# Order of the output stage, the spread of softmax reciprocals and twenty small memsets in a fused attention and GEGLU kernel

## Chip, cores and metric

The kernel runs on one core of a Trainium2 chip. The metric is the device time in microseconds, the median of several runs.

## What is computed

A sequence of 2048 rows of 512 (bf16) is normalised. One branch is attention with 32 heads of 16, in which each position looks at 8 keys, two positions apart, behind it. The other is a gated MLP of width 1792. Their product is added to the input.

```
xn = layernorm(x)
q, k, v = split(xn @ wqkv)                    # 32 heads of 16
idx = pos - 2 * arange(8);  mask = idx >= 0
attn = softmax(where(mask, q . k[idx] / 4, -1e9))
s = (attn . v[idx]) @ wo
y = (gelu(xn @ w_gate) * (xn @ w_up)) @ w_down
out = x + s * silu(y)
```

## The kernel before

The rows are handled in four chunks j of 512 columns (four tiles of 128 rows each). The order of the work is written out by hand: every engine runs its own instructions in the order in which the program emits them. The main loops (L531 to L541) go through, for each chunk, 14 slices of the gated MLP (`glu`, L394), then the 12 projections of the next chunk (`qkv`, L257: four q, four k, four v), then the four output tiles of this chunk (`down`, L407). The pieces of the attention are hung between these with `at(key, fn, ...)`, and `run` emits them ahead of the slice, projection or tile of that key. So `at(("qkv", 1, 10), av_sums, 0)` puts the sums of chunk 0 ahead of projection 10 of chunk 1.

The attention of a chunk goes through these steps:

- `qk_product` (L290): VectorE multiplies q by k shifted by 2w, for each of the 8 taps w, into a buffer `pk`. `pk` and `pv` share eight buffers.
- `logits` (L298): TensorE sums the products over the 16 positions of a head with the constant matrix `dsum` (32 columns wide, four of them side by side on the array) into `L_ps`; ScalarE takes the exponential into `E`. For chunk 0 GpSimd zeroes what lies before the first row.
- `denominators` (L318): TensorE sums `E` over the taps with the constant `hsum`, also 32 columns wide, into `den_ps`; VectorE takes the reciprocal into `rs`, a 128x128 tile.
- `av_product` (L358): VectorE multiplies `E` by the shifted v (`v_arr`, read back from the DRAM tensor `vT` by `load_v`), eight times, into `pv`.
- `av_sums` (L369): TensorE sums these over the taps with `hsum` into `o_ps`, 32 matmuls of 32 columns. The matmuls read the eight products one after the other. `o_ps` and `L_ps` share one PSUM buffer of four banks.
- The reciprocals must be spread from a tile of 128x128 to one of 128x512, `rb`. `spread_by_dma` (L347) does it for chunks 0 to 2: a store of `rs` to the DRAM tile `rs_d`, then four loads. `spread_reciprocals` (L336) does it for chunk 3 with four matmuls by a constant `spread` into `sp_ps` and a copy by ScalarE.
- `divide` (L384): VectorE multiplies `o_ps` by `rb`, in two halves, into `oT`.

`down` computes for a tile of rows y (14 matmuls by w_down) and, directly behind it, s (4 matmuls of `oT` by wo); ScalarE takes silu of y into `sl`; VectorE makes m = s * sl and o_t = m + x; a DMA stores it. The very last tile is done in two halves of 256 columns.

The PSUM pool `mm` has four buffers, which g, u, y, s, the projections, `den_ps` and `sp_ps` take in turn. All DMAs are issued by SyncE (SP), one after the other; an issue that waits holds back those behind it. The constants `dsum`, `hsum` and `spread` are made by GpSimd in `sum_constants` (L145), which is emitted ahead of the second half of the first projections. Before it on GpSimd stand the `pow` of the norms of tiles 4 to 7, behind it those of tiles 8 to 15.

Of the kernel before, what the change touches and what calls it, by code (L numbers as in the profile page):

```python
# [8 lines left out]
ALU = mybir.AluOpType  # L9
AF = mybir.ActivationFunctionType  # L10
BF16 = mybir.dt.bfloat16
F32 = mybir.dt.float32

P = 128
H = 32
# [6 lines left out]
TQ = 512  # L22
# [6 lines left out]
def kernel(  # L29
# [13 lines left out]
    nc = tc.nc  # L43
    B, S, D = A_x.shape
    DF = B_w_gate.shape[1]
    NT, NC, NF, NJ = S // P, D // P, DF // P, S // TQ
    TPQ = TQ // P
    SV = PAD + S
    x2d, out2d = A_x[0], out[0]
# [3 lines left out]
    def pool(name, bufs, **kw):  # L53
        return ctx.enter_context(tc.tile_pool(name=name, bufs=bufs, **kw))

    const = pool("const", 1)
# [8 lines left out]
    op = pool("op", 1)  # L65
    sm = pool("sm", 3)
    sm2 = pool("sm2", 2)
    sm4 = pool("sm4", 4)
    xnp = pool("xnp", 6)
    dram = pool("dram", 1, space=bass.MemoryType.DRAM)  # L70
    mm = pool("mm", 4, space=bass.MemoryType.PSUM)
# [3 lines left out]
    x_sb = big.tile([P, NT, D], BF16, name="x_sb")  # L75
# [3 lines left out]
    wd_sb = wts.tile([P, NF, D], BF16, name="wd_sb")  # L79
    wo_sb = wts.tile([P, NC, D], BF16, name="wo_sb")  # L80
    vT = dram.tile([D, SV], BF16, name="vT")
    rs_d = [dram.tile([P, P], BF16, name=f"rs_d{j}") for j in range(NJ - 1)]

    def load_x(t, n=1):
        nc.sync.dma_start(
# [21 lines left out]
    def load_late_weights():  # L107
# [13 lines left out]
    ident = const.tile([P, P], BF16, name="ident")  # L121
    make_identity(nc, ident[:])
    nc.sync.dma_start(
        out=vT.rearrange("(k p) n -> p k n", p=P)[:, :, 0:PAD],
        in_=zpad[:],
    )

    def band(dst, lo_base, hi_base, step, mult, n):

        nc.gpsimd.affine_select(  # L130
            out=dst, in_=dst, pattern=[[-step, n]], compare_op=ALU.is_ge, fill=0.0,
            base=lo_base, channel_multiplier=mult,
        )
        nc.gpsimd.affine_select(
            out=dst, in_=dst, pattern=[[step, n]], compare_op=ALU.is_gt, fill=0.0,
            base=hi_base, channel_multiplier=-mult,
        )


    hsum = const.tile([P, H], BF16, name="hsum")  # L140
    spread = const.tile([P, 4, P], BF16, name="spread")

    dsum = const.tile([P, NC, H], BF16, name="dsum")

    def sum_constants():  # L145

        nc.gpsimd.memset(dsum[:], 0.0)
        for c in range(NC):
            nc.gpsimd.memset(dsum[:, c, 8 * c : 8 * c + 8], 1.0)
            band(dsum[:, c, 8 * c : 8 * c + 8], 0, 16, 16, 1, 8)  # L150
        for j in range(WL):
            nc.gpsimd.tensor_copy(
                out=hsum[H * j : H * (j + 1), :],
                in_=ident[H * j : H * (j + 1), H * j : H * (j + 1)],
            )
        nc.gpsimd.memset(spread[:], 0.0)
        for q in range(4):
            for j in range(4):
                nc.gpsimd.tensor_copy(
                    out=spread[H * q : H * (q + 1), q, H * j : H * (j + 1)],  # L160
                    in_=ident[H * q : H * (q + 1), H * q : H * (q + 1)],
                )

    xnT = {}
    k_sb = big.tile([P, NC, PAD + S], BF16, name="k_sb")
# [89 lines left out]
    st = [dict(pk={}, pv={}) for _ in range(NJ)]  # L255

    def qkv(j, fo, i0=0, n=TQ, ps=None):  # L257
        which, c = divmod(fo, NC)
        if fo == 0 and i0 == 0:
            st[j]["q"] = qp.tile([P, NC, TQ], BF16, name="q_sb")  # L260
        if ps is None:
            ps = mm.tile([P, n], F32, name="qkv_ps", tag="mm")[:]
            project(ps, wqkv_sb, fo * P, j, i0, n)
        if which == 0:
            nc.scalar.activation(out=st[j]["q"][:, c, i0 : i0 + n], in_=ps, func=AF.Copy)  # L265
        elif which == 1:
            lo = PAD + j * TQ + i0
            nc.scalar.activation(out=k_sb[:, c, lo : lo + n], in_=ps, func=AF.Copy)  # L268
        else:
            vst = sm4.tile([P, TQ], BF16, name="vst")  # L270
            nc.scalar.activation(out=vst[:], in_=ps, func=AF.Copy)  # L271
            lo = PAD + j * TQ
            nc.sync.dma_start(out=vT[c * P : (c + 1) * P, lo : lo + TQ], in_=vst[:])
# [44 lines left out]
    def denominators(j):  # L318
# [14 lines left out]
            nc.vector.reciprocal(out=rs[:], in_=den[:])  # L333
        st[j]["rs"] = rs

    def spread_reciprocals(j):  # L336
        sp = mm.tile([P, TQ], F32, name="sp_ps", tag="mm")
        for q in range(4):
            nc.tensor.matmul(
                sp[:, q * P : (q + 1) * P], lhsT=spread[:, q, :], rhs=st[j]["rs"][:],  # L340
                start=True, stop=True,
            )
        rb = op.tile([P, TQ], F32, name="rb")
        nc.scalar.activation(out=rb[:], in_=sp[:], func=AF.Copy)
        st[j]["rb"] = rb

    def spread_by_dma(j):  # L347

        nc.sync.dma_start(out=rs_d[j][:, :], in_=st[j]["rs"][:])
        rb = op.tile([P, TQ], BF16, name="rbd")  # L350
        for i in range(WL):
            nc.sync.dma_start(
                out=rb[H * i : H * (i + 1), :].rearrange("h (q i) -> h q i", q=4),
                in_=rs_d[j].rearrange("(q h) i -> h q i", h=H),
            )
        st[j]["rb"] = rb
# [47 lines left out]
        nc.vector.tensor_tensor(out=h[:], in0=ge[:], in1=u[:], op=ALU.mult)  # L404
        st[j][fc] = h

    def down(j, tt):  # L407
        t = j * TPQ + tt
        halves = [slice(0, D // 2), slice(D // 2, D)] if t == NT - 1 else [slice(0, D)]
        n = D // len(halves)  # L410
        sl = sm2.tile([P, D], BF16, name="sl")
        o_t = sm4.tile([P, D], BF16, name="o_t")
        for i, cols in enumerate(halves):
            y = mm.tile([P, n], F32, name="y_ps", tag="mm")
            for fc in range(NF):
                nc.tensor.matmul(  # L416
                    y[:],
                    lhsT=st[j][fc][:, tt * P : (tt + 1) * P],
                    rhs=wd_sb[:, fc, cols],
                    start=(fc == 0),  # L420
                    stop=(fc == NF - 1),
                )
            nc.scalar.activation(out=sl[:, cols], in_=y[:], func=AF.Silu)  # L423
            s = mm.tile([P, n], F32, name="s_ps", tag="mm")
            for g in range(NC):
                nc.tensor.matmul(  # L426
                    s[:],
                    lhsT=st[j]["oT"][:, g, tt * P : (tt + 1) * P],
                    rhs=wo_sb[:, g, cols],
                    start=(g == 0),  # L430
                    stop=(g == NC - 1),
                )
            m = sm2.tile([P, n], BF16, name="m")
            nc.vector.tensor_tensor(out=m[:], in0=s[:], in1=sl[:, cols], op=ALU.mult)  # L434
            nc.vector.tensor_tensor(out=o_t[:, cols], in0=m[:], in1=x_sb[:, t, cols], op=ALU.add)
            nc.sync.dma_start(out=out2d[t * P : (t + 1) * P, cols], in_=o_t[:, cols])


    side = {}
# [1 line left out]
    def at(key, fn, *args):  # L441
        side.setdefault(key, []).append((fn, args))

    def run(stage, j, i):
        for fn, args in side.get((stage, j, i), ()):
            fn(*args)
# [13 lines left out]
        at(("glu", 0, w), qk_product, 0, w)  # L460
    at(("glu", 0, 9), logits, 0)
    for i in range(8):
        at(("glu", 0, 12 + i) if i < 2 else ("qkv", 1, (0, 1, 3, 4, 5, 6)[i - 2]),
           av_product, 0, i // 2, i % 2)
    at(("qkv", 1, 3), denominators, 0)
    at(("qkv", 1, 3), spread_by_dma, 0)
    at(("qkv", 1, 10), av_sums, 0)
    at(("qkv", 1, 10), divide, 0)

    for j in range(1, NJ):  # L470
        for w in range(W):
            early = j > 1 and w < 3
            at(("qkv", j, 9 + w) if early else ("down", j - 1, w // 3), qk_product, j, w)
        for i in range(TPQ):
            at(("down", j - 1, i), load_v, j, [i])
        at(("glu", j, 0), logits, j)
        for i in range(8):
            at(("glu", j, 2 + i), av_product, j, i // 2, i % 2)
        at(("glu", j, 11), denominators, j)
        at(("glu", j, 11), av_sums, j)  # L480
        if j + 1 < NJ:
            at(("glu", j, 11), spread_by_dma, j)
            at(("qkv", j + 1, 6), divide, j)
        else:
            at(("glu", j, 12), spread_reciprocals, j)
            at(("glu", j, 13), divide, j)


    HT = TPQ // 2
# [41 lines left out]
    for j in range(NJ):  # L531
        for fc in range(NF):
            run("glu", j, fc)
            glu(j, fc)
        if j + 1 < NJ:
            for i in range(12):
                run("qkv", j + 1, i)
                qkv(j + 1, i)
        for tt in range(TPQ):
            run("down", j, tt)  # L540
            down(j, tt)  # L541
# [1 line left out]
_INS = ['A_x', 'A_wqkv', 'A_wo', 'B_x', 'B_w_gate', 'B_w_up', 'B_w_down']  # L543
_OUTS = [((1, 2048, 512), 'bfloat16')]
# [25 lines left out]
```

The softmax here doesn't subtract the row's maximum and nothing guards it: scores larger than these inputs give would overflow.

## Time and profile before

| | |
|---|---|
| median of 5 runs | 230.37 us (229.94 to 230.49) |
| profiled execution | 230.1 us |
| its span in the profile | 228.4 us |
| mean granted TensorE clock | 0.998 |
| DMA moved | 24.46 MB |

The profile shows one execution. Times in it are microseconds from the start of the span. PE is TensorE's matmul, PEld its weight load, DVE VectorE, ACT ScalarE, POOL GpSimd, SP SyncE; SPq is SP's DMA queue. A row of a timeline has the start, the time covered, the engine, the line of the program, the operation, the tile written and the tiles read, and, in brackets, how long the engine had been idle and what ended that. The chain of waits follows the work that ended last back to the start. The last matmul group of the timeline, an s of 256 columns, starts at 224.25, and the last o_t on VectorE at 225.42. The stores of the reciprocals have 32 KB each and landed in a median of 1.5 us, the twelve loads of rbd in 1.6 to 2.1 us, the stores of vT (128 KB each) in 1.7 to 8.3, the loads of v_arr (520 KB each) in 4.8 to 12.2 with a median of 5.1.

### The profile page before, as it was taken

To read this page: it belongs to the slowest core of one execution; us is meant where nothing else is said; L and a number is where in the kernel's file an instruction comes from. 1 tells how busy PE (TensorE), PEld (TensorE's weight loads), DVE (VectorE), ACT (ScalarE), POOL (GpSimd) and SP (SyncE) were. 2 spreads that over 40 slices of the span, in tenths; PEclk is the share of its full clock that TensorE was granted. 3 is DMA by queue.
4 is the path that set the end of the run, shared out by engine and by line. 5 is a ranking of instruction groups with operands and counts; after the bars stand their busy time and mean duration, and the time that the engine had idled before them with its cause. 6 is when DMAs were issued, how large, how long until landed. Compare 5 with 4: busy or idle time off the path is not lost.

```text
span 228.4 us, 3538 instructions
## 1 busy us (share of the span) xinstructions
PE 223.7 (98%) x1324; PEld 106.6 (47%) x1324; DVE 147.7 (65%) x234; ACT 130.1 (57%) x214; POOL 22.0 (10%) x61
## 2 busy tenths in 40 slices
PE   8999999999999999999999999999999999999993
PEld 6864444444444444444444444444444444444453
DVE  4693996896994298864687179635549429945232
ACT  3779769764413876467621786747632396748211
POOL 1058943000000000110000000000000000000000
PEclk9999999999999999999999999999999999999999
DMA  5999589982468111110287511110147800000001
GB/s 171 357 372 373 135 170 197 234 219 72 120 159 207 45 25 28 26 29 0 92 185 158 138 25 29 26 35 0 46 128 160 202 27 0 0 0 4 23 23 46
DMA packets 30545, 24.46 MB, mean 107 GB/s; under 512 B 10176, under 2 KB 30528, under 8 KB 30528
## 3 DMA queue, kind: packets, MB, share of 16 engines
q1 hardware_dynamic: 30528, 24.24, 41.7%
q8 instruction: 10, 0.16, 0.3%
q14 instruction: 7, 0.06, 0.1%
HBM read 18.61 MB, written 4.31 MB: 100 GB/s over the span
## 4 chain that ended last, share of the span: by engine, by line
PE 96%; ACT 2%; DVE 0%; issue 0%; DVEq 0%
PE y_ps L416 21%; PE u_ps L247 21%; PE g_ps L247 21%; PE qkv_ps L247 18%; PE s_ps L426 6%; PE L_ps L304 3%; PE o_ps L375 3%; PE warm_ps L229 2%; PE q_ps L247 1%; ACT xnT L221 1%; ACT L400 1%; PE tr L212 0%; PE den_ps L324 0%; ACT ge L400 0%; ACT vst L271 0%; DVE m L434 0%
## 5 line engine op out<-in xcount | busy, mean ns | idle before, releaser
L247 PE MATMUL g_ps<-xnT,wg_sb 128*128 128x512 bf16 x224 | 57.6, 379 | 0.0
L247 PE MATMUL u_ps<-xnT,wu_sb 128*128 128x512 bf16 x224 | 57.5, 379 | 0.0
L416 PE MATMUL y_ps<-wd_sb,h 128*128 128x512 bf16 (+1 forms) x238 | 51.2, 366 | 0.0
L404 DVE TENSOR_TENSOR h<-ge,u 128x512 bf16<-128x512 bf16 x56 | 23.8, 425 | 37.2 <-ACT u L402 36.6
L293 DVE TENSOR_TENSOR pk<-q_sb,k_sb 128x2048 bf16<-128x2048 bf16 x32 | 37.8, 1220 | 7.0 <-ACT k_sb L268 7.0
L402 ACT ACTIVATE u<-u_ps 128x512 bf16<-128x512 f32 x56 | 33.5, 599 | 14.7 <-PE u_ps L247 14.7
L400 ACT ACTIVATE ge<-g_ps 128x512 bf16<-128x512 f32 x56 | 33.5, 598 | 14.7 <-PE g_ps L247 14.4
L247 PE MATMUL qkv_ps<-xnT,wqkv_sb 128*128 128x512 bf16 (+1 forms) x208 | 40.9, 355 | 0.0
L361 DVE TENSOR_TENSOR pv<-E,v_arr 128x2048 bf16<-128x2048 bf16 x32 | 38.6, 1217 | 0.0
L416 PEld LDWEIGHTS <-h 128*128 128x128 bf16 x238 | 23.3, 98 | 25.3
L423 ACT ACTIVATE sl<-y_ps 128x512 bf16<-128x512 f32 (+1 forms) x17 | 9.7, 572 | 44.0 <-PE y_ps L416 44.0
L247 PEld LDWEIGHTS <-wu_sb 128*128 128x128 bf16 x224 | 21.9, 98 | 26.7 <-issue 0.3
L247 PEld LDWEIGHTS <-wg_sb 128*128 128x128 bf16 x224 | 21.2, 98 | 27.1 <-issue 3.0
L247 PEld LDWEIGHTS <-wqkv_sb 128*128 128x128 bf16 x224 | 21.7, 98 | 19.7 <-issue 0.7
L434 DVE TENSOR_TENSOR m<-s_ps,sl 128x512 bf16<-128x512 f32 (+1 forms) x17 | 11.2, 658 | 24.2 <-PE s_ps L426 24.1
L426 PE MATMUL s_ps<-wo_sb,oT 128*128 128x512 bf16 (+1 forms) x68 | 16.6, 366 | 0.0
L197 POOL TENSOR_TENSOR rstd<-rstd,mhalf 128x1 f32<-128x1 f32 x12 | 7.6, 636 | 78.0 <-DVE rstd L194 75.8
L271 ACT ACTIVATE vst<-qkv_ps 128x512 bf16<-128x512 f32 x16 | 9.6, 597 | 6.4 <-PE qkv_ps L247 6.4
L268 ACT ACTIVATE k_sb<-qkv_ps 128x512 bf16<-128x512 f32 (+1 forms) x20 | 10.1, 516 | 3.5 <-PE qkv_ps L247 3.2
L265 ACT ACTIVATE q_sb<-qkv_ps 128x512 bf16<-128x512 f32 (+1 forms) x16 | 8.7, 544 | 3.6 <-PE qkv_ps L247 3.3
L426 PEld LDWEIGHTS <-oT 128*128 128x128 bf16 x68 | 6.6, 98 | 7.2
L192 DVE BATCH_NORM_STATS2 stats<-x_sb 128x6 f32<-128x512 bf16 x12 | 8.2, 686 | 1.3 <-DMA x_sb<-in_A_x_dram 1.3
(52 smaller groups left out, 116.8 us busy)
## 6 DMA issues: line engine op xcount, KB each, us to landing
v_arr<-vT SPq DMA_DIRECT2D x16, 520.0 KB, 5.1
vT<-vst SPq DMA_DIRECT2D x16, 128.0 KB, 2.5
out_dram<-o_t SPq DMA_DIRECT2D x15, 128.0 KB, 1.9
wg_sb<-in_B_w_gate_dram SPq DMA_DIRECT2D x2, 896.0 KB, 10.8
wu_sb<-in_B_w_up_dram SPq DMA_DIRECT2D x2, 896.0 KB, 12.9
wd_sb<-in_B_w_down_dram SPq DMA_DIRECT2D x1, 1792.0 KB, 14.0
wqkv_sb<-in_A_wqkv_dram SPq DMA_DIRECT2D x3, 512.0 KB, 4.9
x_sb<-in_A_x_dram SPq DMA_DIRECT2D x3, 512.0 KB, 12.0
```

The costliest lines, as they stand in the source:

```text
L247: nc.tensor.matmul(ps, lhsT=w[:, dk, lo : lo + P], rhs=xnT[j][:, dk, i0 : i0 + n], start=(dk == 0), stop=(dk == NC - 1),)
L268: nc.scalar.activation(out=k_sb[:, c, lo : lo + n], in_=ps, func=AF.Copy)
L271: nc.scalar.activation(out=vst[:], in_=ps, func=AF.Copy)
L293: nc.vector.tensor_tensor(out=pk[:], in0=st[j]["q"][:], in1=k_sb[:, :, off : off + TQ], op=ALU.mult)
L361: nc.vector.tensor_tensor(out=pv[:], in0=st[j]["E"][:, wh, :].unsqueeze(1).to_broadcast([P, 4, TQ]), in1=st[j]["va"][:, 4 * g : 4 * g + 4, ...
L400: nc.scalar.activation(out=ge[:], in_=g_ps[:], func=AF.Gelu_apprx_tanh)
L402: nc.scalar.activation(out=u[:], in_=u_ps[:], func=AF.Copy)
L404: nc.vector.tensor_tensor(out=h[:], in0=ge[:], in1=u[:], op=ALU.mult)
L416: nc.tensor.matmul(y[:], lhsT=st[j][fc][:, tt * P : (tt + 1) * P], rhs=wd_sb[:, fc, cols], start=(fc == 0), stop=(fc == NF - 1),)
L423: nc.scalar.activation(out=sl[:, cols], in_=y[:], func=AF.Silu)
L426: nc.tensor.matmul(s[:], lhsT=st[j]["oT"][:, g, tt * P : (tt + 1) * P], rhs=wo_sb[:, g, cols], start=(g == 0), stop=(g == NC - 1),)
L434: nc.vector.tensor_tensor(out=m[:], in0=s[:], in1=sl[:, cols], op=ALU.mult)
```

## The change

- y and s are split into `down` and `finish`. y of a tile is followed by s of the tile before it; s of a chunk's last tile follows its y. In the last tile of all, y of the first half is followed by s of tile 14 and then by its own s.
- The reciprocals of all four chunks go by DRAM. The function with the matmuls is gone, with the constant `spread`. The store and the four loads are now two functions. In chunk 0 the store is emitted ahead of projection 8 and the loads ahead of projection 10, so that the vT stores of projections 8 and 9 stand between them on SP.
- In chunk 0 `denominators` moves from projection 3 to 8 and `av_sums` from 10 to 8, directly behind it. The products of chunk 0 begin a slice earlier, ahead of glu 11, and end ahead of projection 5 instead of 6.
- The divide of chunk 0 moves from projection 10 to the first output tile, that of chunk 3 from glu 13 to the first output tile. Those of chunks 1 and 2 stay.
- The first three pk products of chunk 1 move from the first output tile to projections 9 to 11, as chunks 2 and 3 have them.
- `sl` now has three buffers of its own (two before), and `o_t` is made for the columns it needs.
- GpSimd gets twenty memsets of one element per partition, all into one tile `filler`, ahead of `dsum`. In the compiled program the first waits for nothing, and each of the other nineteen waits for GpSimd's own previous instruction.

```diff
-    rs_d = [dram.tile([P, P], BF16, name=f"rs_d{j}") for j in range(NJ - 1)]
+    rs_d = [dram.tile([P, P], BF16, name=f"rs_d{j}") for j in range(NJ)]
...
-    spread = const.tile([P, 4, P], BF16, name="spread")
-
     dsum = const.tile([P, NC, H], BF16, name="dsum")
 
+    filler = const.tile([P, 1], F32, name="filler")
+
     def sum_constants():
+
+        for _ in range(20):
+            nc.gpsimd.memset(filler[:], 0.0)
 
         nc.gpsimd.memset(dsum[:], 0.0)
...
-        nc.gpsimd.memset(spread[:], 0.0)
-        for q in range(4):
-            for j in range(4):
-                nc.gpsimd.tensor_copy(
-                    out=spread[H * q : H * (q + 1), q, H * j : H * (j + 1)],
-                    in_=ident[H * q : H * (q + 1), H * q : H * (q + 1)],
-                )
...
+    def store_reciprocals(j):
+        nc.sync.dma_start(out=rs_d[j][:, :], in_=st[j]["rs"][:])
+
     def spread_reciprocals(j):
-        sp = mm.tile([P, TQ], F32, name="sp_ps", tag="mm")
-        for q in range(4):
-            nc.tensor.matmul(
-                sp[:, q * P : (q + 1) * P], lhsT=spread[:, q, :], rhs=st[j]["rs"][:],
-                start=True, stop=True,
-            )
-        rb = op.tile([P, TQ], F32, name="rb")
-        nc.scalar.activation(out=rb[:], in_=sp[:], func=AF.Copy)
-        st[j]["rb"] = rb
-
-    def spread_by_dma(j):
-
-        nc.sync.dma_start(out=rs_d[j][:, :], in_=st[j]["rs"][:])
-        rb = op.tile([P, TQ], BF16, name="rbd")
+
+        rb = op.tile([P, TQ], BF16, name="rb")
         for i in range(WL):
             nc.sync.dma_start(
...
+    def down(j, tt, cols):
+
+        n = cols.stop - cols.start
+        y = mm.tile([P, n], F32, name="y_ps", tag="mm")
...
+        sl = sm.tile([P, n], BF16, name="sl")
+        nc.scalar.activation(out=sl[:], in_=y[:], func=AF.Silu)
+        return sl
+
+    def finish(j, tt, cols, sl):
+
+        t, n = j * TPQ + tt, cols.stop - cols.start
+        s = mm.tile([P, n], F32, name="s_ps", tag="mm")
...
+        m = sm2.tile([P, n], BF16, name="m")
+        nc.vector.tensor_tensor(out=m[:], in0=s[:], in1=sl[:], op=ALU.mult)
+        o_t = sm4.tile([P, n], BF16, name="o_t")
+        nc.vector.tensor_tensor(out=o_t[:], in0=m[:], in1=x_sb[:, t, cols], op=ALU.add)
+        nc.sync.dma_start(out=out2d[t * P : (t + 1) * P, cols], in_=o_t[:])
...
-        at(("glu", 0, 12 + i) if i < 2 else ("qkv", 1, (0, 1, 3, 4, 5, 6)[i - 2]),
+        at(("glu", 0, 11 + i) if i < 3 else ("qkv", 1, (0, 1, 2, 4, 5)[i - 3]),
            av_product, 0, i // 2, i % 2)
-    at(("qkv", 1, 3), denominators, 0)
-    at(("qkv", 1, 3), spread_by_dma, 0)
-    at(("qkv", 1, 10), av_sums, 0)
-    at(("qkv", 1, 10), divide, 0)
+    at(("qkv", 1, 8), denominators, 0)
+    at(("qkv", 1, 8), av_sums, 0)
+    at(("qkv", 1, 8), store_reciprocals, 0)
+    at(("qkv", 1, 10), spread_reciprocals, 0)
+    at(("down", 0, 0), divide, 0)
 
     for j in range(1, NJ):
         for w in range(W):
-            early = j > 1 and w < 3
-            at(("qkv", j, 9 + w) if early else ("down", j - 1, w // 3), qk_product, j, w)
+            at(("qkv", j, 9 + w) if w < 3 else ("down", j - 1, w // 3), qk_product, j, w)
...
-        if j + 1 < NJ:
-            at(("glu", j, 11), spread_by_dma, j)
-            at(("qkv", j + 1, 6), divide, j)
-        else:
-            at(("glu", j, 12), spread_reciprocals, j)
-            at(("glu", j, 13), divide, j)
+        at(("glu", j, 11), store_reciprocals, j)
+        at(("glu", j, 11), spread_reciprocals, j)
+        at(("qkv", j + 1, 6) if j + 1 < NJ else ("down", j, 0), divide, j)
...
+        todo = []
         for tt in range(TPQ):
             run("down", j, tt)
-            down(j, tt)
+            last = j * TPQ + tt == NT - 1
+            for cols in (slice(0, D // 2), slice(D // 2, D)) if last else (slice(0, D),):
+                sl = down(j, tt, cols)
+                if todo:
+                    finish(*todo.pop())
+                if last:
+                    finish(j, tt, cols, sl)
+                else:
+                    todo.append((j, tt, cols, sl))
+        if todo:
+            finish(*todo.pop())
```

More of the change, by code (lines that the diff above doesn't have):

```diff
@@ L405, in glu @@
         st[j][fc] = h
[L407 to L436, printed above, removed]
@@ new lines, in down @@
+    def down(j, tt, cols):
+        n = cols.stop - cols.start
+        y = mm.tile([P, n], F32, name="y_ps", tag="mm")
+        for fc in range(NF):
+            nc.tensor.matmul(
+                y[:],
+                lhsT=st[j][fc][:, tt * P : (tt + 1) * P],
+                rhs=wd_sb[:, fc, cols],
+                start=(fc == 0),
+                stop=(fc == NF - 1),
+            )
+        sl = sm.tile([P, n], BF16, name="sl")
+        nc.scalar.activation(out=sl[:], in_=y[:], func=AF.Silu)
+        return sl
@@ new lines, in finish @@
+    def finish(j, tt, cols, sl):
+        t, n = j * TPQ + tt, cols.stop - cols.start
+        s = mm.tile([P, n], F32, name="s_ps", tag="mm")
+        for g in range(NC):
+            nc.tensor.matmul(
+                s[:],
+                lhsT=st[j]["oT"][:, g, tt * P : (tt + 1) * P],
+                rhs=wo_sb[:, g, cols],
+                start=(g == 0),
+                stop=(g == NC - 1),
+            )
+        m = sm2.tile([P, n], BF16, name="m")
[3 more added lines that the diff above has]
+        nc.sync.dma_start(out=out2d[t * P : (t + 1) * P, cols], in_=o_t[:])
```

## The prediction, as put on record before the run

> **What bounds the kernel now.** I read the page first, then the waits, then the chain of waits in two short windows, then the timelines of VectorE (DVE), GpSimd (POOL) and the DMA queue of SyncE (SP) around the places that the diff touches.
>
> ```profile
> span 228.4 us, 3538 instructions
> PE 223.7 (98%) x1324; PEld 106.6 (47%) x1324; DVE 147.7 (65%) x234; ACT 130.1 (57%) x214; POOL 22.0 (10%) x61
> PE 96%; ACT 2%; DVE 0%; issue 0%; DVEq 0%
> ```
>
> TensorE (PE) is busy for 98% of the span and is 96% of the chain that ended last. No other engine is above 65%. PE's waits, in full, are 0.8 us before the warm-up and 0.3 us before the first q. A 128x512 matmul follows another every 0.216 us: the chain shows 14 of them in 3.02 us for every y and 4 in 0.86 us for every s. So there is no gap between y and s to close. A change pays only by the matmuls it takes from PE's line, or by what PE loses at a seam. The seams are in the chain, first in chunk 0, then in chunk 3:
>
> ```profile
> 44.53 2.59 PE qkv_ps L247 x12
> 47.12 0.23 PE den_ps L324 x8
> 47.35 6.15 PE qkv_ps L247 x28
> 53.50 1.84 PE o_ps L375 x32
> 55.34 1.83 PE qkv_ps L247 x8
> ```
>
> ```profile
> 201.81 0.23 PE den_ps L324 x8
> 202.03 1.73 PE o_ps L375 x32
> 203.76 0.97 PE g_ps L247 x4
> 204.73 0.86 PE u_ps L247 x4
> 205.59 0.22 PE sp_ps L339 x4
> 205.81 0.86 PE g_ps L247 x4
> ```
>
> The columns are start, duration, group. Twenty-eight matmuls at 0.216 make 6.05, not 6.15; eight make 1.73, not 1.83; four make 0.86, not 0.97. About 0.10 us is lost in each group that follows a group of the other shape (full 128x128 against the 32-column tiles of den, o and L).
>
> [...]some 0.10 us each time, and none between den and o, which share a mode (o takes 1.73 after den, 1.84 after qkv). [...]an affine select took 1.07 us under a pk product (16.85 to 17.92), and 0.19 at its other places. Of a memset beside a product it shows nothing; I rest only a bound on it.
>
> **The change, part by part.**
>
> *Reciprocals of chunk 3 by DRAM.* This removes four sp_ps matmuls from PE, 0.22 us in the chain, and ScalarE's copy to rb (0.59 us, under PE). It adds one store and four loads on SP, which has no transfer to issue between chunk 2's last output and 214.44. In chunk 0 before, 0.97 us passed from the start of the reciprocal (49.27) to the store, 1.51 to the first load, 1.75 for four issues, and a load lands in at most 2.1. The last of the four is issued 0.43 us before their end. So from 202.87 rb is there by 202.87 + 0.97 + 1.51 + 1.32 + 2.1 = 208.8. The divide now stands behind h of the last slice, whose u is copied by 209.96; h frees VectorE at 210.3, and the divide takes 2.35, to 212.7. The first s now follows two y, at 209.10 + 6.04 = 215.1. Slack 2.4; cost nothing. If that cover failed, s would wait the excess.
>
> *den of chunk 0 joined to its o.* Before: seam of den inside the qkv row (0.10 after it), a seam into o (0.11) and one out (0.10), den itself 0.23. Joined, as chunk 3 does it: 0.23 + 1.73 + 0.11. The sum 0.23 + 0.10 + 1.84 + 0.10 = 2.27 becomes 2.07: 0.20 us saved.
>
> *Is VectorE in time for the earlier sums?* o moves up two qkv slots, and one product moves up with the rest. These rows set it:
>
> ```profile
> 42.25 0.41 DVE L203 TENSOR_SCALAR xn<-x_sb,mv,rstd 128x512 bf16<-128x512 bf16 x1 [0.75 <-POOL rstd L197]
> 42.58 0.42 DVE L404 TENSOR_TENSOR h<-ge,u 128x512 bf16<-128x512 bf16 x1
> 42.92 1.22 DVE L361 TENSOR_TENSOR pv<-E,v_arr 128x2048 bf16<-128x2048 bf16 x1
> 49.27 0.95 DVE L333 RECIPROCAL rs<-den_ps 128x128 bf16<-128x128 f32 x1
> 50.13 3.42 DVE L361 TENSOR_TENSOR pv<-E,v_arr 128x2048 bf16<-128x2048 bf16 x3
> ```
>
> VectorE runs without a pause from 42.25 to 53.55. The reciprocal (0.86 from its start to the next) now comes after the eighth product, which ends at 53.55 - 0.86 = 52.69. On PE, eight qkv slots from 44.37 (timeline) end at 44.37 + 32 x 0.216 = 51.28; seam 0.09, den 0.12, o from 51.49; its last eighth, the one that reads that product, starts 7 x 0.216 later, at 53.00. Slack 0.3 us, which was about 1.4 before. The first product may now start at 42.58 instead of 42.92; the last of its v_arr loads was issued near 30.1 and the slowest took 12.2 us to land, so until about 42.3. This is the tightest place of the change. I take no stall; the bounds are 0 and, if the loads are 0.6 us later, 0.3.
>
> *rb of chunk 0 and the divide.* On SP the store is followed by two vT stores, which wait for vst of slots 8 and 9, and only then by the four loads. A vT store went out 1.71 us after the start of its slot on PE (55.27 to 56.98). Slot 8 now starts when o ends, 53.33, slot 9 at 54.19; their stores go at 55.04 and 55.90, the loads from 56.24, the last at 57.56, and rb is there by 59.7. VectorE first does three pk products (to 56.9), waits, and divides to 60.9 (first half) and 62.0. y starts at 53.33 + 4 x 0.864 = 56.79, two of them end at 62.83, and s reads the second half with its third matmul at 63.26. Slack 1.3. Had s stayed directly behind y, at 59.8, it would have stalled; the reordering covers the longer way. Behind the waiting divide stand three pk (65.4), m and o_t (66.4), two pk (68.8); L reads these from 72.4, slack 3.6.
>
> *s one tile behind y elsewhere.* The same matmuls in another order, so 0 on PE. Four PSUM buffers go round: s of tile 0 is freed by m at about 66.1 and its buffer is asked for by s of tile 2 at 70.6. In chunks 1 and 2 nothing else moves but one or two products on VectorE, idle there for 2.7 us per tile. In the last tile y of the first half is followed by s of tile 14 (0.86); its m and o_t (1.1 us on VectorE) are done during the last y (1.53). The tail after the last s keeps its length.
>
> *Twenty memsets, less the spread constants.*
>
> ```profile
> 16.07 0.20 POOL L147 MEMSET dsum<- 128x128 bf16 x1
> 17.87 0.10 POOL L149 MEMSET dsum<- 128x8 bf16 x1
> 18.04 0.19 POOL L130 TENSOR_SCALAR_AFFINE_SELECT dsum<-dsum 128x8 bf16<-128x8 bf16 x1
> 21.15 8.84 POOL L159 COPY spread<-ident 32x32 bf16<-32x32 bf16 x16
> 33.88 1.91 PE L304 MATMUL L_ps<-pk,dsum 128*32 128x512 bf16 x32
> ```
>
> All twenty write one tile, and nineteen wait for the one before. A memset and a waiting successor are 0.17 apart (17.87 to 18.04), so 20 x 0.17 = 3.4 us; the four memsets of constants at the start, without a wait, are 0.034 apart, which gives 0.7. Upwards, 1.07 each (the blocked select) would be 21.4, [...]VectorE is idle from 17.9 to 21.3. dsum, ready at 19.62, is ready by 23.0; with some selects now under pk products (one blocked copy took up to 1.2 us) perhaps 27. L needs it at 33.88. The copies removed (8.84) and the memset before them (0.52) outweigh the addition, so GpSimd is also free before tile 8's rstd at 32.8. Cost 0.
>
> **The sum.** 0.22 + 0.20 = 0.42 us off PE's line. The profiled execution took 230.1 us (span 228.4 and 1.7 around it) and would take 229.68. The median of five is 230.37, 0.27 above the profiled one: 230.37 - 0.42 = 229.95, or 0.18% less.
>
> **Rivals.**
> (a) The sums of chunk 0 wait for the last product, because v_arr lands later or VectorE's chain is longer than I add up. For it: only 0.3 us are left, behind loads that took up to 12.2 us. Against it: all my terms are measured ones. A stall of 0.3 gives 230.25.
> (b) More is gained than the trace shows. The unprofiled median is 0.27 above the profiled time, so other executions may lose time at places this trace passes freely (v_arr in chunk 0, the divide before the last h in chunk 3, 0.6 us before y asks for that h). If the order relieves that, 0.42 + 0.4 gives 229.55. Against it: four of five runs lie within 0.14 us.
> (c) Slower: rb of chunk 0 is late, and s waits on PE with everything behind it. If the loads, sharing the engines with two vT stores, land in 5.1 us (the median of v_arr's loads) instead of 2.1, rb is there at 62.7, the divide ends at 65.0 and s waits 65.0 - 63.26 = 1.7 us: 230.37 - 0.42 + 1.7 = 231.65. It eats the gain once rb comes after 61.4. For it: the path is 3.8 us longer behind the reciprocal than it was bare. Against it: twelve rb loads landed in 1.6 to 2.1.
> dsum coming too late needs 0.71 us for each memset ((33.88 - 19.62) / 20); I count it under (c)'s share.
>
> **Chances.** A measurement of this kernel can tell about 0.2% from no change, that is 0.46 us: below 229.91 is faster, above 230.83 slower. The forecast has 0.70, spread by some 0.15 us about 229.95, so 0.31 of it below 229.91 and 0.39 above; (a) 0.11, within; (b) 0.12, faster; (c) 0.07, slower. Faster 0.43, same 0.50, slower 0.07. The range goes from (b), 229.45, to somewhat over (a), 230.55; (c) and a tail of (b) stay out.
>
> **What the profile after should show.** No sp_ps row; den directly ahead of o in chunk 0, o 1.73 in the chain; the start of the first y some 0.2 us earlier than 57.01, that of the last s 0.42 earlier than 224.25; PE waits as before, without o_ps or s_ps among them. oT of chunk 0 starts near 59.7, with an idle VectorE before it. dsum is ready before 28 and L starts at 33.88 as before. I am wrong if PE waits for pv, oT or dsum, or if a seam remains where den joined o.

## The result and the profile after

The changed kernel takes 229.59 us (median of 25 runs, 229.36 to 230.10), the kernel before, beside it, 230.15 us (46 runs, 229.90 to 230.78). The ratio is 0.9974, with a 95% interval of 0.9969 to 0.9980: 0.26% faster, or 0.60 us (0.46 to 0.71) of 230.15. The two medians are 0.56 us apart. The sum of the prediction was 0.42 us.

The head of the page of the changed kernel:

```profile
span 228.3 us, 3535 instructions
PE 223.9 (98%) x1320; PEld 107.0 (47%) x1320; DVE 147.7 (65%) x234; ACT 129.7 (57%) x213; POOL 15.0 (7%) x64
PE 97%; ACT 1%; DVE 0%; issue 0%; DVEq 0%
```

Four matmuls and a copy of ScalarE are gone, and GpSimd's work fell by 7 us. But the profiled execution took 229.99 us, hardly less than the 230.1 before. The chain of waits around the sums of chunk 0 seems to say that time was lost:

```profile
44.97 6.91 PE qkv_ps L243 x32
51.88 0.23 PE den_ps L320 x8
52.10 1.73 PE o_ps L362 x32
53.83 3.56 PE qkv_ps L243 x16
57.39 4.75 PE y_ps L399 x22
```

The seams are gone as predicted: 32 matmuls in 6.91 (0.216 each), o in 1.73 behind den, 3.56 for 16 with one seam. Yet y starts at 57.39, 0.22 later than the end of the row of projections before (55.34 + 1.83 = 57.17). The reason is at the other end. TensorE's timeline, first of the kernel before, then of the changed one:

```profile
5.83 0.38 PE L212 MATMUL tr<-ident,xn 128*128 128x128 bf16 x4
6.72 1.91 PE L247 MATMUL q_ps<-xnT,wqkv_sb 128*128 128x256 bf16 x16 [0.28 <-ACT xnT L221]
...
224.25 0.60 PE L426 MATMUL s_ps<-wo_sb,oT 128*128 128x256 bf16 x4
```

```profile
6.05 0.63 PE L208 MATMUL tr<-ident,xn 128*128 128x128 bf16 x4
...
7.16 1.91 PE L243 MATMUL q_ps<-xnT,wqkv_sb 128*128 128x256 bf16 x16
...
224.26 0.60 PE L415 MATMUL s_ps<-wo_sb,oT 128*128 128x256 bf16 x4
```

The first q started 0.44 us later in this execution, because the second transposes and the warm-ups beside them still ran at 107 ns each (start to start in the trace's records), where those of the other execution ran at 56. The trace also records the granted clock: its full rate begins at 6.83 us in this execution and at 5.58 in the other. So the two spans cannot be compared from their starts. From the first q to the last s it is 224.25 - 6.72 = 217.53 us before and 224.26 - 7.16 = 217.10 after: 0.43 us less, against 0.42 predicted. I use this stretch for all kernels below. The first q starts between 6.51 and 7.23 us in the fourteen profiles of this study, and it follows that record: 6.51 to 6.68 in the six where the full rate begins by 4.5 us, 6.72 to 6.84 in the five where it begins between 5.5 and 6.4, and 7.16 to 7.23 in the three where it begins after 6.6. The point lay between 3.5 and 6.9 us in the fourteen, and 0.72 us of that range reaches the first q. Why it moves from one execution to the next was not shown.

In chunk 3 the spread matmuls have left the chain:

```profile
202.26 1.73 PE o_ps L362 x32
203.99 0.97 PE g_ps L243 x4
204.96 0.86 PE u_ps L243 x4
205.82 0.86 PE g_ps L243 x4
```

VectorE and GpSimd, at the rows that the prediction used:

```profile
42.71 1.22 DVE L348 TENSOR_TENSOR pv<-E,v_arr 128x2048 bf16<-128x2048 bf16 x1
...
47.12 5.76 DVE L348 TENSOR_TENSOR pv<-E,v_arr 128x2048 bf16<-128x2048 bf16 x5
52.80 0.95 DVE L329 RECIPROCAL rs<-den_ps 128x128 bf16<-128x128 f32 x1
53.67 3.43 DVE L289 TENSOR_TENSOR pk<-q_sb,k_sb 128x2048 bf16<-128x2048 bf16 x3
60.08 2.36 DVE L374 TENSOR_TENSOR oT<-o_ps,rb 128x1024 bf16<-128x1024 f32 x2 [2.99 <-DMA rb<-rs_d]
```

```profile
15.66 3.30 POOL L148 MEMSET filler<- 128x1 f32 x20
18.89 0.20 POOL L150 MEMSET dsum<- 128x128 bf16 x1
...
21.44 1.96 POOL L155 COPY hsum<-ident 32x32 bf16<-32x32 bf16 x4
```

The divide of chunk 0 waits 2.99 us for rb; a wait was forecast, and nobody waits for the divide. The memsets take 3.30 us (forecast 3.4), and dsum is ready at 21.4. PE waits for neither.

### The profile page after: what moved, and what is told of

The parts are those of the page before. It is cut to its first block, busy times and chain, and to the rows that moved or that the text cites. A ratio compares the mean times of both kernels' runs of the same rounds, so it can differ in the third digit from the quotient of the medians.

```text
span 228.3 us, 3535 instructions
## 1 busy us (share of the span) xinstructions
PE 223.9 (98%) x1320; PEld 107.0 (47%) x1320; DVE 147.7 (65%) x234; ACT 129.7 (57%) x213; POOL 15.0 (7%) x64
## 3 DMA queue, kind: packets, MB, share of 16 engines
q1 hardware_dynamic: 31248, 24.41, 42.4%
## 4 chain that ended last, share of the span: by engine, by line
PE 97%; ACT 1%; DVE 0%; issue 0%; DVEq 0%
PE y_ps L399 21%; PE u_ps L243 21%; PE g_ps L243 21%; PE qkv_ps L243 17%; PE s_ps L415 6%; PE L_ps L300 3%; PE o_ps L362 3%; PE warm_ps L225 2%; PE q_ps L243 1%; PE tr L208 1%; ACT L387 1%; PE den_ps L320 0%; ACT xnT L217 0%; ACT ge L387 0%; ACT vst L267 0%; DVE m L423 0%
## 5 line engine op out<-in xcount | busy, mean ns | idle before, releaser
L399 PE MATMUL y_ps<-wd_sb,h 128*128 128x512 bf16 (+1 forms) x238 | 50.5, 366 | 0.0
L415 PE MATMUL s_ps<-wo_sb,oT 128*128 128x512 bf16 (+1 forms) x68 | 15.9, 366 | 0.0
L374 DVE TENSOR_TENSOR oT<-o_ps,rb 128x1024 bf16<-128x1024 f32 x8 | 9.4, 1218 | 3.0 <-DMA rb<-rs_d 3.0
```

What stands on the lines that cost most here:

```text
L399: nc.tensor.matmul(y[:], lhsT=st[j][fc][:, tt * P : (tt + 1) * P], rhs=wd_sb[:, fc, cols], start=(fc == 0), stop=(fc == NF - 1),)
L415: nc.tensor.matmul(s[:], lhsT=st[j]["oT"][:, g, tt * P : (tt + 1) * P], rhs=wo_sb[:, g, cols], start=(g == 0), stop=(g == NC - 1),)
```

## The experiments

Each is the changed kernel with one edit, if not said otherwise. "q to s" is the time from the start of the first q to the start of the last s in the profile. "Outside" is the profiled execution's time less its span. The load rate is what the DMAs moved between 15 and 20 us, when weights and x are loaded. Every kernel was timed beside the kernel before on the same chip, and its ratio is to those runs. The last three columns are from one profile of each kernel. e5 and e6 with 120 memsets ran twice each, e6 with 60 six times, the others 9 to 25 times. The intervals of e3 and e4 overlap that of the changed kernel; what tells these apart is the stretch from q to s and the chain.

| kernel | ratio (95%) | median, before beside it | q to s | outside | load rate GB/s |
|---|---|---|---|---|---|
| before | | | 217.53 | 1.7 | 368 |
| changed | 0.9974 (0.9969 to 0.9980) | 229.59, 230.15 | 217.10 | 1.7 | 399 |
| e1 memsets alone | 0.9997 (0.9987 to 1.0007) | 230.29, 230.24 | 217.55 | 1.7 | 397 |
| e2 no memsets | 0.9980 (0.9972 to 0.9989) | 229.87, 230.24 | 217.09 | 2.0 | 371 |
| e3 spread matmuls back | 0.9986 (0.9975 to 0.9997) | 229.89, 230.24 | 217.34 | 1.7 | 399 |
| e4 den apart | 0.9983 (0.9971 to 0.9995) | 229.88, 230.24 | 217.41 | 1.7 | 398 |
| e5 s behind its y | 1.0058 (1.0035 to 1.0080) | 231.70, 230.31 | 219.19 | 1.7 | 396 |
| e6 60 memsets | 0.9970 (0.9957 to 0.9983) | 229.67, 230.31 | 217.10 | 1.7 | 398 |
| e6 120 memsets | 1.0143 (1.0121 to 1.0165) | 233.66, 230.31 | 221.10 | 1.7 | 398 |
| e7 no memsets, no warm-ups between | 0.9988 (0.9981 to 0.9994) | 230.05, 230.31 | 217.52 | 2.0 | 370 |
| e8 memsets at the end | 0.9980 (0.9973 to 0.9987) | 229.67, 230.17 | 217.17 | 1.7 | 397 |
| e9 no memsets, sums a slot later | 0.9990 (0.9981 to 0.9999) | 229.87, 230.17 | 217.42 | 1.8 | 369 |
| e10 as e9, no warm-ups between | 0.9995 (0.9981 to 1.0009) | 229.88, 230.17 | 217.09 | 2.0 | 370 |
| e11 with memsets, sums a slot later | 0.9976 (0.9967 to 0.9986) | 229.65, 230.17 | 217.14 | 1.7 | 399 |

**e1, the memsets alone**, in the kernel before.

```diff
+    filler = const.tile([P, 1], F32, name="filler")
     def sum_constants():
+        for _ in range(20):
+            nc.gpsimd.memset(filler[:], 0.0)
```

> The kernel before with the twenty memsets added and nothing else. Theory (the gain is 0.22 us of spread matmuls and 0.20 us of seams; GpSimd's constants are off the path): ratio to before 1.000, within 0.05%; dsum ready near 23 us or a little later, L starts at 33.9 or, if the first q starts late, up to 0.45 later. Rival (the memsets hold GpSimd up until dsum or the norms of tile 8 are late): a wait of PE before L and a ratio above 1.001.

Measured: 0.9997, q to s 217.55 against 217.53, no wait of PE before L. In the kernel before, no cost of the memsets can be seen.

**e2, the change without the memsets** (the tile `filler` and the loop taken out).

> The changed kernel without the twenty memsets. Theory: the same time as the changed kernel, ratio to before 0.9974 to 0.998. Rival (the memsets cost something that the other parts had to pay for): lower than the changed kernel by over 0.1%, ratio under 0.9965. The opposite rival (the memsets bring part of the gain[...]): ratio above 0.9985.

Measured: q to s as in the changed kernel (217.09), and a ratio inside the first range. But the median stands only 0.37 us under the kernel before, where the changed kernel stands 0.56 under it. The two intervals overlap; the column "outside" gave a hint, and e8 to e11 take it up.

**e3, the spread matmuls back** in chunk 3.

```diff
-        at(("glu", j, 11), store_reciprocals, j)
-        at(("glu", j, 11), spread_reciprocals, j)
+        if j + 1 < NJ:
+            at(("glu", j, 11), store_reciprocals, j)
+            at(("glu", j, 11), spread_reciprocals, j)
+        else:
+            at(("glu", j, 12), spread_by_matmul, j)
```

> The changed kernel with chunk 3's reciprocals spread by the four matmuls and ScalarE's copy again (constant spread included), the divide left at the first output tile. Theory: 0.22 us of the gain is given back, about 0.1% above the changed kernel: ratio to before near 0.9985; sp_ps 0.22 in the chain. Rival (the gain lies elsewhere, the matmuls were in a gap): as the changed kernel, 0.9974.

Measured: 0.9986 and q to s 217.34, that is 0.24 more. The lowest time is 0.23 us under the lowest of the kernel before, where that of the changed kernel is 0.54 under it. The chain of e3 has the row again, between u and g, which keep their 0.86:

```profile
204.35 0.86 PE u_ps L252 x4
205.22 0.22 PE sp_ps L357 x4
205.44 0.86 PE g_ps L252 x4
```

**e4, den apart from o** in chunk 0.

```diff
-    at(("qkv", 1, 8), denominators, 0)
+    at(("qkv", 1, 3), denominators, 0)
```

> The changed kernel with the denominators of chunk 0 ahead of projection 3 again; sums, store and loads stay where the change put them. Theory: two seams come back, 0.20 us: ratio to before near 0.9984; den 0.23 followed by 0.10 lost in the projections, o 1.84. Rival (seams are paid once however the groups stand): as the changed kernel.

Measured: 0.9983 and q to s 217.41, 0.31 more, not 0.20; the lowest time is 0.27 us under that of the kernel before. The chain of e4 tells the two parts:

```profile
47.64 0.23 PE den_ps L320 x8
47.86 4.42 PE qkv_ps L243 x20
52.29 1.93 PE o_ps L362 x32
54.21 3.56 PE qkv_ps L243 x16
```

The 20 projections take 0.10 more than 20 x 0.216, the seam behind den. o takes 1.93, not 1.84. With den early, the reciprocal stands on VectorE ahead of the last products again; that the 0.09 is o's wait for the last one is my estimate, from these two figures. The remaining 0.21 or so is the seams, which were priced at 0.20.

**e5, s directly behind its own y.**

```diff
-                if last:
+                if True:
                     finish(j, tt, cols, sl)
```

> The changed kernel with each s directly behind its own y. Theory: the divide of chunk 0 is not done when s is asked for: y ends near 60.0, the second half of oT is there at about 62.4, and s reads it with its third matmul: PE waits 1.8 to 2.0 us there, and in chunk 3 another 0.1 to 0.3; together about 2 us, 231.5 to 232 us, and the waits of PE show s_ps on oT. Rival (the reordering covers nothing; the loads come in time anyway): no wait, the time of the changed kernel.

Measured: 231.70 us, ratio 1.0058; q to s 219.19, 2.09 more than with the change. TensorE's timeline shows s waiting for each half of oT in chunk 0:

```profile
61.02 0.60 PE L415 MATMUL s_ps<-wo_sb,oT 128*128 128x512 bf16 x2 [1.02 <-DVE oT L374]
62.15 0.60 PE L415 MATMUL s_ps<-wo_sb,oT 128*128 128x512 bf16 x2 [0.53 <-DVE oT L374]
```

Counted from start to start, s is 1.88 us late in chunk 0 (due at 59.84, and its third matmul at 61.45), and 0.19 in chunk 3, where four matmuls take 1.05 instead of 0.86. So without the order the longer way of the reciprocals costs five times what the change gains. No run has the order alone; e3 and e4 account for all of the 0.43, which leaves nothing for it to gain by itself.

**e6, 60 and 120 memsets.**

```diff
-        for _ in range(20):
+        for _ in range(120):
```

> The changed kernel with 60 memsets instead of 20. At 0.165 us each they end at about 25.6; dsum follows under the pk products by 29 to 33. Theory: no wait before L (33.5 to 33.9), the time of the changed kernel. Rival (some other work waits for GpSimd, or the slack is smaller): over 0.3 us more.

> The changed kernel with 120 memsets instead of 20. They end at about 35.5, dsum follows by 38 to 40, L was due at 33.5 to 33.9. Theory: PE waits 4 to 6 us before L and the time grows by as much, to 234 to 236. Rival (dsum is not on the path even then): as the changed kernel.

Measured: with 60, dsum is done at 32.1, q to s is that of 20, no wait. With 120 they end at 34.8, and PE's waits have:

```profile
PE L_ps L300 <- POOL dsum L152: 2.0, 3, 1.7
```

The time is 233.66, and q to s is 4.00 more than in the changed kernel, at the lower end of the 4 to 6 expected. But only about 2.4 of it is the wait. L is released in four steps, one for each quarter of dsum: its first matmul was due at 33.99 and started at 35.73, and the second and third steps lost some 0.35 each. The rest is TensorE's clock, which fell to half behind these waits, as a line of the windows shows (the third number from the end is the granted clock):

```profile
36.60:40.01 3.41, 3.24 (x29) 0.85 (x26) 1.02 (x3) 0.11 (x1) 1.94 (x9) 0.50 1.21 176
```

From the start of the last 24 matmuls of L to the u behind them 3.83 us pass, where the changed kernel takes 2.28. The expectation had the size right, but not this part of it. So the way from the memsets to TensorE is there, and 20 of them have some 12 us of slack before it. A memset took 0.16 us in each of these kernels (3.30 for 20, 9.58 for 60, 18.98 for 120). The selects behind the 60, between 26 and 32 us, took up to 1.07, where the same ones took 0.19 behind the 120.

**e7, no memsets and no warm-ups between the transposes.**

```diff
-    warm_up(4, P)
     transpose(1, parts=2)
-    warm_up(4, P)
```

> The changed kernel without the memsets and without the two groups of four warm-up matmuls beside the second transposes. In the profile of the changed kernel the first q started 0.44 us later than in the one before: its early warm-ups and transposes ran at 107 ns each instead of 56. If these warm-ups only hold the transposes back, the first q starts up to 0.4 earlier when they run slow, and the mean falls by 0.1 to 0.3 us against the kernel with them. If they are needed to keep TensorE at speed, later matmuls run slow and the time grows.

Measured: the first q at 6.58 is early, but that is about as early as in e3, e8, e9 and e11 with the warm-ups. The time did not fall: 0.9988. In its profile q to s is 217.52; the 0.42 us of the change is all lost in chunk 0. VectorE's timeline and the chain of waits of e7:

```profile
43.05 1.23 DVE L343 TENSOR_TENSOR pv<-E,v_arr 128x2048 bf16<-128x2048 bf16 x1 [0.83 <-DMA v_arr<-vT]
```

```profile
47.55 4.26 DVE pv L343 x4
...
52.01 1.23 DVE pv L343
...
53.28 0.40 PE o_ps L357 x4
```

The first product waits for v_arr until 43.05 (42.71 in the changed kernel's profile, on a TensorE that was 0.58 us later), and the last eighth of o for the last product. This is rival (a), on record with 0.11. In this profile TensorE was early and v_arr late at once: by the trace's records the last v_arr landed at 42.8, and at 41.3 in the profile of the changed kernel. The wait may be the rule in e7: its 22 executions have spans of 228.0 or more, where those of e2 begin at 227.7 and those of e10, with a slot more, at 227.8.

After e1 to e7 one thing stood out. In the profiles without the memsets the loads at the start are slower (368 to 371 GB/s against 396 to 399), and v_arr is later: its last load lands at 42.3 to 42.8, and with them by 41.6, but for e3 (42.4). The rates differ before any of the memsets runs: between 10 and 15 us they are 375 to 380 and 395 to 404, and the first memset of the changed kernel starts at 15.66. e8 to e11 ask what that has to do with the memsets, and whether more slack pays.

**e8, the memsets at the end** of GpSimd's program.

```diff
-        for _ in range(20):
-            nc.gpsimd.memset(filler[:], 0.0)
...
+    def late_memsets():
+        for _ in range(20):
+            nc.gpsimd.memset(filler[:], 0.0)
+
+    at(("glu", 2, 2), late_memsets)
```

> The changed kernel with its twenty memsets moved to the end of GpSimd's program (glu slice 2 of chunk 2, where nothing on GpSimd follows). So far the three profiles of kernels without the memsets show 368 to 371 GB/s between 15 and 20 us and the last load of v_arr landed at 42.3 to 42.8; the seven with them show 396 to 399 GB/s and, but for one, 41.1 to 41.6. The rate differs before the memsets run (from 5 us on). If it goes with the program and not with what GpSimd does at 16 us, this kernel shows 396 to 399 and the time of the changed kernel (ratio 0.997 to 0.9975); if the memsets' place matters, it shows 370 and the time of the kernel without them (0.998 or above). If it shows either without a change of the time, the rate isn't what makes the difference of the two.

Measured: 397 GB/s, median 0.50 us below the kernel before beside it. The ratio, 0.9980, is the one expected if the place mattered; its interval holds the changed kernel's 0.9974 as well, so the ratio does not decide. The rate does, and so does the column "outside": 1.67 to 1.78 us in all 17 executions, as with the memsets in their first place (below). Two lines of the windows, e8 and then e9, which has no memsets (the last number is the load rate):

```profile
15.00:20.00 5.00, 5.00 (x31) 2.52 (x30) 2.73 (x7) 4.01 (x6) 3.94 (x17) 1.00 1.05 397
```

```profile
15.00:20.00 5.00, 5.00 (x31) 2.50 (x30) 3.57 (x10) 4.03 (x6) 3.73 (x14) 1.00 1.06 369
```

So the rate isn't set by what GpSimd does at 16 us. It goes with the program.

**e9, sums a slot later, no memsets; e10, the same without the warm-ups; e11, sums a slot later, with memsets.**

```diff
-    at(("qkv", 1, 8), denominators, 0)
-    at(("qkv", 1, 8), av_sums, 0)
-    at(("qkv", 1, 8), store_reciprocals, 0)
+    at(("qkv", 1, 9), denominators, 0)
+    at(("qkv", 1, 9), av_sums, 0)
+    at(("qkv", 1, 9), store_reciprocals, 0)
```

> The changed kernel without the memsets, with denominators, sums and store of chunk 0 ahead of projection 9 instead of 8. Theory (in executions with an early start the sums of chunk 0 wait for products that wait for v_arr, 0.3 to 0.4 us; one slot later gives 0.86 us of slack; the loads go out behind the vT store of slot 9 as before): o has no wait in the profile, the lowest times fall from 229.66 to about 229.4, the median to 229.6 or under, ratio 0.997. Rival (the products were in time, the difference to the changed kernel is chance): as without the memsets, lowest 229.66, ratio 0.998.

> The same, also without the two groups of four warm-up matmuls beside the second transposes. Theory: without them the first q started early in the profile, and that kernel lost 0.42 us to the wait of the sums; with the wait covered, most executions are near 229.4 to 229.6, ratio 0.9965 to 0.997. Rival (the start is no earlier on the whole): as the kernel with the warm-ups.

> The changed kernel, memsets included, with denominators, sums and store of chunk 0 ahead of projection 9. Theory: with the memsets v_arr is there by 41.6 and the sums hardly waited, so it is within 0.05% of the changed kernel, and within 0.05% of the same kernel without the memsets: with the slack the memsets make no difference. Rival (the memsets help in another way): 0.1% below the kernel without them.

Measured: e9 did not do what I expected. In its profile o still takes 1.91 (1.73 without a wait), and v_arr had landed only at 43.5. Its lowest time is 229.58, its median 229.87, as without the extra slack (e2, 229.87); e10 has 229.88. e11, which differs from e9 by `filler` and the memsets alone, has 229.65 beside it on the same chip, 0.22 us less. My theory that the sums' wait makes the difference between the kernels with and without memsets falls, and so does its other half, that with the slack the memsets make none. e11 is not distinguishable from the changed kernel, so no version here beats it.

What the four changed kernels without memsets (e2, e7, e9, e10) share is the column "outside": 1.8 to 2.0 us, against 1.7 in all ten others. The record has the span of every execution, so this can be looked at beyond the profiles. Time less span is 1.66 to 1.79 us in all 132 executions of the kernel before that ran beside the experiments, and in all 108 of the kernels with memsets. In the four it is over 1.8 in 63 of 71 executions, up to 2.11, with medians of 1.88 to 1.99. The spans themselves hardly differ: a median of 228.0 in e9 and 227.9 in e11. So the 0.22 us lies outside the span.

In those four, and in none of the others, the trace has a transfer of instructions after the end of the span. The DMA view of e2 from 228 to 232 us, where its span ends at 228.3:

```profile
DMA packets 1, 0.01 MB, mean 2 GB/s; under 512 B 0, under 2 KB 0, under 8 KB 0
## 3 DMA queue, kind: packets, MB, share of 16 engines
q14 instruction: 1, 0.01, 0.7%
```

It is one packet of 8 KB that starts at 230.2. The same view of the changed kernel and of the one before is empty. GpSimd's busy line counts 44 instructions in those four and 61 to 164 in the ten others. By the traces' records every profile has seven such packets of 8 KB behind the start of the span. In the ten, one of them starts at 23.7 to 23.9 us where GpSimd has 81 or more instructions (four kernels), and at 43.8 to 45.8 where it has 61 to 64 (six). The four have none at these places, and theirs starts at 229.8 to 230.2. So it looks like one and the same fetch, and its place goes with the length of GpSimd's program. The kernel before, with neither memsets nor `filler` but 61 instructions, is among the ten, which speaks for the number of instructions and against the tile. That the packet belongs to GpSimd is inferred from these counts, the record has no engine; why it starts so late with 44 instructions was not shown. Nor does any run show that the end of the execution waits for it.

## Why the prediction held, and where it was short

The forecast, 229.95 us in 229.45 to 230.55, held with 229.59, and its two sources of gain are shown. The miss of 0.36 us has two parts. The point stood on a median of five runs, 230.37; 46 runs beside the changed kernel gave 230.15, and from there the sum leads to 229.73. The other 0.14 is the size of the change, which was forecast too small. The range took in both because it was 1.1 us wide. The likeliest outcome of the prediction, no change that can be told (0.50), did not come: 229.59 lies below its own limit of 229.91, to which it gave 0.43.

- *Spread matmuls, 0.22.* e3 gives 0.24 in q to s. Their replacement by DRAM cost nothing: the last load landed at 209.41 by the trace's records, and the divide of chunk 3 ran from 210.34, directly behind h, as forecast.
- *Joining den to o, 0.20.* The chain shows o at 1.73 and one seam less on either side; e4 gives 0.21 once the 0.09 that I put down to a wait is set apart. The changed kernel has 0.43 less from q to s, against 0.42 forecast. The first y and the last s were forecast 0.2 and 0.42 earlier. Counted from the first q they are (0.22 and 0.43); on the clock of the profile they are not, because the prediction took the start of TensorE for fixed.
- *rb of chunk 0.* Forecast for 59.7; oT started at 60.08 with a q that was 0.44 later, 59.64 on the old clock. e5 shows what its cover was worth, 2.1 us, and rival (c) did not come. Its "3.8 us longer" does not come out of the prediction's own terms: from the start of the reciprocal to rb these add to 5.9 bare and to 7.0 with the two stores between, 1.1 more. The profile has 7.3; on SP the four loads begin at 56.74, behind the two vT stores (55.46 to 56.64).
- *The tightest place.* No stall was taken, and the changed kernel's profile has none. The slack was judged rightly as thin: e7 and, by 0.18 us, e9 show rival (a) at work. The changed kernel's profile had a late TensorE, which helps; but e8, the same order with an early one (first q at 6.61) and v_arr at 41.2, has no wait either. How often other executions meet it was not measured.
- *Memsets, 0.* Right for the engines: e1, e6 with 60, and e8 leave q to s within 0.07 of where it was. They were priced only by what waits for GpSimd, and an effect outside that price was missed. Without the twenty memsets the change would have left GpSimd with 44 instructions, and some 0.2 us (e11 against e9) would have been paid outside the span. With them, this doesn't arise. So the removal of `spread` had a price and the memsets paid it: the zero of the sum is the right net by luck, for a reason that the prediction didn't have.
- *The size.* The measured 0.60 (0.46 to 0.71) is more than 0.42, so a term is missing. One is found in the profiles: the prediction let the tail keep its length, and the tail got shorter. By the traces' records 2.63 us pass from the issue of the last output to the end of the span in the kernel before, and 2.54 in the changed one. SP's last waits look at the DMA semaphores in a fixed order, 0.06 us apart. Before, the one that the last output fills was in the second look, and four more looks and a drain stood behind it; after, with five more transfers ahead of it, it was in the third, with three behind it. e1 and e3, which lack the transfers in chunk 3, end as the kernel before (2.64 and 2.63); the ten others have 2.52 to 2.55. 0.43 and 0.09 make 0.52, inside the interval. The lowest times, 229.90 before and 229.36 after, are 0.54 apart, and the lower quartiles 0.52. What goes beyond lies in the slower executions: the upper quartiles, 230.49 and 229.78, are 0.71 apart. There the start of TensorE may play a part, which moves an execution by up to 0.7 us, but no profile of such an execution was taken, and I cannot assign this rest.

Rival (b), more than the trace shows, had that direction. Its reason, places where other executions lose time and this order relieves them, is neither shown nor ruled out: the kernel before has one profile, of 230.1 us, and its upper quartile is 230.49.

Still open: why the loads run at 396 to 399 GB/s in the nine profiles of kernels with memsets and at 368 to 371 in the five without. Those kernels also have the tile `filler`, which shifts the tiles loaded behind it by 32 bytes in each partition: in the compiled programs x_sb starts at byte 77312 of a partition with it and 77280 without, at 78336 in e1 and e3 and 78304 in the kernel before. Whether the start or the instructions set the rate wasn't tried; a kernel with the tile and no memsets would tell. For the time of the kernel before it mattered little: e1 has the higher rate and no gain. In the changed one a late v_arr can cost (e7).

## What to carry to other kernels

When one engine is 98% busy with matmuls that never wait, look for what it does needlessly: matmuls that a DMA can stand in for, and groups of another shape (here of 32 columns among those of 128) that stand alone, at some 0.1 us for each seam. The detour by DRAM cost nothing with other work between its two ends and 2.09 us without (e5), so first move the consumer back (here s behind the next y), and take stock of what gets tight elsewhere, by the latest landing that a trace shows and not by its usual one. For effects of a few tenths of a microsecond compare stretches between the same two instructions, and look outside the span too.

## What the runs showed that was not expected

- The execution's start moves: the first q came between 6.51 and 7.23 us in fourteen profiles, with the start of the full clock in the trace's record, and the rest of TensorE's work moved with it.
- With twenty instructions fewer on an engine that nobody waits for, what lies outside the span rose from 1.7 us to a median of 1.9 to 2.0, together with a fetch of 8 KB of instructions that came after the end of the span.
- The load rate at the start stood at two levels, 368 to 371 and 396 to 399 GB/s, by program and not by execution, as far as fourteen profiles tell.
- The place of the last output among SP's final waits is worth some 0.09 us.
- A wait of TensorE cost more than the wait: with 120 memsets some 2.4 us of waiting were followed by 3.41 us at half the granted clock, which cost about 1.6 more.
